# LayerNorm statistics of five token tiles as two accumulating passes on ScalarE, two more product groups in the first projection, five more warm-up matmuls

## Chip, cores, metric

One core of a Trainium2 chip. The metric is the device time of one execution in microseconds (us), the median of several runs.

## The reference, cut to what matters

```python
def _A_ref(x, wqkv, wo):                 # attention layer, linear attention, 32 heads of 32
    q, k, v = split_heads(x @ wqkv)      # x: 2048 x 1024, wqkv: 1024 x 3072
    phi = lambda t: where(t > 0, t + 1, exp(t)) + 1e-6
    pq, pk = phi(q), phi(k)
    kv, z = einsum(pk, v), sum(pk)
    return (pq @ kv / (pq @ z + 1e-6)) @ wo

x = x + _A_ref(_layernorm(x), ...)       # layer one: the only layer that the change touches
x = x + _B_ref(_layernorm(x), ...)       # gated bilinear unit
x = x + _A_ref(_layernorm(x), ...)       # layer three, same weights
x = x + _B_ref(_layernorm(x), ...)
```

## The kernel before: the parts concerned

The 2048 tokens are 16 tiles of 128. In layer one each tile is loaded, its LayerNorm statistics are taken, it is normalised and transposed, and then projected to k and q. A recorder (`P.add`) puts every operation into the in-order queue of its engine and derives the waits. The cuts below are shortened: `...` stands for dependence lists, and the loads of x and the branches for other layers are left out. The statistics take three operations on VectorE and two small ones on GpSimd:

```python
def ln_a(i):                              # statistics of tile i into mv[j]
    for h in range(2):
        P.add("dve", lambda e: e.bn_stats(st[j][:, 6*h:6*h+6], x_res[:, i, half h]), ...)
    P.add("dve", lambda e: e.bn_aggr(mv[j][:, 0:2], st[j]), ...)                     # mean, variance
    P.add("pool", lambda e: e.tensor_scalar(out=mv[j][:, 2:3], in0=mv[j][:, 1:2], scalar1=EPS_LN, op0=ALU.add), ...)
    P.add("pool", lambda e: e.tensor_tensor(out=mv[j][:, 3:4], in0=mv[j][:, 2:3], in1=mhalf, op=ALU.pow), ...)

def ln_b2(i, j, dst, ...):                # normalise: (x - mean) * rstd
    P.add("dve", lambda e: e.tensor_scalar(out=dst, in0=x_res[:, i, :], scalar1=mv[j][:, 0:1],
                                           scalar2=mv[j][:, 3:4], op0=ALU.subtract, op1=ALU.mult), ...)

def lnstep(i, h):                         # between two half projections of a tile
    if h == 0:
        lnp.start(lnp.n)                  # statistics of the next tile
        lnp.b_one()                       # normalise the one before it
    else:
        lnp.step_t(1)                     # transpose it
```

A plain projection takes 8 matmuls of 512 columns for each tile, each of k and q and each half of the columns. Its PSUM bank is evicted by an exp and a relu on ScalarE and by two operations on VectorE; four banks are used in turn. Ten tiles are projected so. For the others two tiles at a time are projected by a 2 x 2 block scheme with seven products instead of eight (28 matmuls instead of 32), which needs extra block sums and two more evictions from VectorE.

```python
PE_WARM = 10           # matmuls on zeros ahead of everything
NPL1 = 10              # tiles projected plainly; the rest in groups of seven products
LNX = (3, 5, 6)        # q projections after which a further statistics step stands
```

Of the kernel before, what the change touches and what calls it, by code (L numbers as in the profile page):

```python
# [7 lines left out]
AF = mybir.ActivationFunctionType  # L8
# [172 lines left out]
def build_kernel(nc, A_x, A_wqkv, A_wo, B_w_gate, B_w_up, B_w_down, out):  # L181
    _, S, D = A_x.shape
    F = B_w_gate.shape[1]
    NST, NSB, KT, NG, NFT, NDH = S // 128, S // 512, D // 128, D // 128, F // 128, D // 512
# [4 lines left out]
    EPS_LN = 1e-5  # L189
    PHI0 = 1e-6  # L190
    PHI1 = 1.0 + 1e-6
    PE_WARM = 10
    NHOLD = 2
    NPL1 = 10
    LNX = (3, 5, 6)
    RLB = [(4, 5, 6, 7), (4, 5, 6, 7)]
    NPE_T = 4
    NNORM = 14
# [20 lines left out]
    def take(n, align=64):  # L219
        nonlocal off  # L220
        off = (off + align - 1) // align * align
        o = off
        off += n
        return o
# [11 lines left out]
    O_MV = [take(64) for _ in range(8)]  # L236
# [21 lines left out]
    O_A = [RC + 2 * SZ_W + 1024 + i * D * 2 for i in range(2)]  # L258
# [25 lines left out]
    P = _Prog(V_TW + 8 * 32)  # L284
# [38 lines left out]
    with ExitStack() as es:  # L323
# [10 lines left out]
        def vb(o, n):  # L334
            return ab[:, o // 2: o // 2 + n]

        def vh(o, n):
            return ah[:, o // 2: o // 2 + n]

        def vf(o, n):  # L340
            return af[:, o // 4: o // 4 + n]

        x_res = vb(O_X, NST * D).rearrange("p (i d) -> p i d", d=D)
# [23 lines left out]
        xn = [vh(o, D) for o in O_XN]  # L367
        asb = [vh(o, D) for o in O_A]
        st = [vf(o, 12) for o in O_ST]
        mv = [vf(o, 5) for o in O_MV]  # L370
        pbufs = [vf(o, D) for o in O_P]
        den = vf(O_DEN, 32)
        rden = [vf(o, 32) for o in O_RDEN]
# [6 lines left out]
        def psb(b):  # L380
            return ps[:, b, :]
# [7 lines left out]
        B_KVT = [1, 2]  # L389
# [16 lines left out]
        def R(o, n):  # L406
            return [(o, o + n)]

        def r_x(i, lo=0, hi=D):
            return [(O_X + (i * D + lo) * 2, O_X + (i * D + hi) * 2)]  # L410
# [16 lines left out]
        def mset(ap, v, rng):  # L427
            P.add("pool", lambda e: e.memset(ap, v), wr=rng)

        wrm = vh(O_A[0], 512)  # L430
        mset(wrm, 0.0, R(O_A[0], 1024))
        P.add("pe", lambda e: [e.matmul(psb(B_KVT[1]), wrm[:, 0:128], wrm, start=True, stop=True) for _ in range(PE_WARM)],
              rd=R(O_A[0], 1024), pwr=[B_KVT[1]])
# [4 lines left out]
        for h in range(4):  # L438
# [4 lines left out]
              rd=R(O_IDENT, 256), wr=R(O_IDENT, 256))  # L443
        P.add("pool", lambda e: e.tensor_copy(e0, ident[:, 0:2]), rd=R(O_IDENT, 256), wr=R(O_E0, 4))

        ln_cnt = [0]

        def ln_a(i):
            j = ln_cnt[0] % 8
            ln_cnt[0] += 1  # L450
            for h in range(2):
                P.add("dve", (lambda h: lambda e: e.bn_stats(st[j][:, 6 * h:6 * h + 6], x_res[:, i, (D // 2) * h:(D // 2) * (h + 1)]))(h),  # L452
                      rd=r_x(i, (D // 2) * h, (D // 2) * (h + 1)), wr=R(O_ST[j] + 24 * h, 24))
            P.add("dve", lambda e: e.bn_aggr(mv[j][:, 0:2], st[j]), rd=R(O_ST[j], 48), wr=R(O_MV[j], 8))  # L454
            P.add("pool", lambda e: e.tensor_scalar(out=mv[j][:, 2:3], in0=mv[j][:, 1:2], scalar1=EPS_LN, scalar2=None, op0=ALU.add),  # L455
                  rd=R(O_MV[j] + 4, 4), wr=R(O_MV[j] + 8, 4))
            P.add("pool", lambda e: e.tensor_tensor(out=mv[j][:, 3:4], in0=mv[j][:, 2:3], in1=mhalf, op=ALU.pow),
                  rd=R(O_MV[j] + 8, 4) + R(O_MHALF, 4), wr=R(O_MV[j] + 12, 4))
            return j

        def ln_b1(i, j, on_act):
            if on_act:
                P.add("dve", lambda e: e.tensor_scalar(out=mv[j][:, 4:5], in0=mv[j][:, 0:1], scalar1=mv[j][:, 3:4], scalar2=-1.0,
                                                        op0=ALU.mult, op1=ALU.mult),
                      rd=R(O_MV[j], 4) + R(O_MV[j] + 12, 4), wr=R(O_MV[j] + 16, 4))
# [10 lines left out]
        class LN:  # L476

            def __init__(self, to, order):
                self.to = to
                self.order = order  # L480
                self.q_b = []
                self.q_n = []
                self.q_t = []
                self.n = 0
                self.t_next = 0
                self.use_dma = False
                self.on_act = False
# [6 lines left out]

            def start(self, i):
                assert i == self.n
                j = ln_a(self.order[i])
                self.n += 1
                self.q_b.append((i, j))

            def b1_one(self):
                if self.q_b:
                    i, j = self.q_b.pop(0)
                    ln_b1(self.order[i], j, self.on_act)
                    self.q_n.append((i, j, self.on_act))

# [169 lines left out]
        def tw_make(n, eng, parts):  # L676
            b11, b12, b21, b22 = [w_blk(n, kb, h) for kb in range(2) for h in range(2)]
            t1, t2, t3, t4 = [tw_blk(n, c) for c in (1, 2, 3, 4)]
            step = 4 // parts
            ops = []  # L680
            for o, a, b in ((t1, b12, b11), (t2, b22, t1), (t4, b21, t2), (t3, b22, b12)):
                for k in range(0, 4, step):
                    def one(o=o, a=a, b=b, k=k):
                        P.add(eng, lambda e: e.tensor_tensor(out=o[0][:, k:k + step], in0=a[0][:, k:k + step], in1=b[0][:, k:k + step], op=ALU.subtract),
                              rd=rsub(a[1], k, step) + rsub(b[1], k, step), wr=rsub(o[1], k, step))
                    ops.append(one)
            return ops
# [33 lines left out]
        def pack():  # L721
            u = pk_n[0]
            if u >= NU:
                return
            pk_n[0] += 1
            assert RG.get("n", 0) <= u, (RG["n"], u)
            j, m = unit_jm(u)
            w16 = wscr[u].bitcast(BF16)[:, 0:2048].rearrange("p (i k c) -> p i k c", i=2, c=128)
            for i in range(2):
                c0 = j * 256 + (1 - i) * 128  # L730
                dma(w16[:, i], wgu_v[m][:, :, c0:c0 + 128], R(V_PK + u * 64 + 32 * i, 32), KPK[u])
# [134 lines left out]
        def xload(i):  # L866
            dma(x_res[:, i, :], x2[i * 128:(i + 1) * 128, :], r_x(i), KX[i])

        def layer_A(lnp, nxt, first):
# [167 lines left out]
            def lnstep(i, h):  # L1037
                if h == 0:
                    if first and lnp.n < NST:
                        for t in (lnp.n, lnp.n + 1):  # L1040
                            if xnext[0] <= t < NST:
                                xload(t)
                                xnext[0] = t + 1
                    if lnp.n < NST:
                        lnp.start(lnp.n)
                    lnp.b_one()
                else:
                    lnp.use_dma = i + 1 >= NPE_T
                    lnp.step_t(1)

            if first:
                lnp.start(0)
                lnp.b_one()
                lnp.step_t(1)
                lnp.start(1)
                lnp.b_one()
            else:
                lnp.use_dma = True
            NPL = NPL1 if first else 0
            rl.update(on=first, o=O_XN[0] if first else O_XRT[tok[NST - 2]])  # L1060
            twk = []
            if first:
                twk = tw_make("k", "dve", 1)
                twq = tw_make("q", "dve", 1)
# [10 lines left out]
            for kind, i in seq:  # L1075
                for h in range(2):
                    ev = proj(kind, tok[i], h, mids.pop((kind, i, h), None) if first else None)
                    ev()
                    if lead:
                        for f in lead.pop(0):  # L1080
                            f()
                        if i == NHOLD:
                            twk.pop(0)()
                    elif kind == "k":
                        lnstep(i, h)
                if kind == "q" and len(twk) > 1:
                    twk.pop(0)()
                elif kind == "q" and i >= 1 and len(twq) > 1:
                    twq.pop(0)()
                if kind == "q" and NPL < NST and i in LNX:  # L1090
                    for h in range(2):
                        lnstep(NPE_T, h)
                if kind == "q" and i >= NPL - 2:
                    if i == NPL - 2:
                        lnp.need(NPL + 1)
                    for f in s_make(tok, NPL // 2)[2 * (i - NPL + 2):][:2]:
                        f()
                if i >= 3 and kind == "k":
                    pack()
# [19 lines left out]
            for n, (kind, p) in enumerate(items):  # L1119
# [10 lines left out]
                if first:  # L1130
                    i = NPL + len(LNX) + n
                    for j in range(2):
# [837 lines left out]
```

## Time and profile before

| | before |
|---|---|
| median, range | 1436.09 us, 1435.76 to 1439.31 (3 runs) |
| TensorE / VectorE / ScalarE busy | 99% / 85% / 47% of the span |
| first projection matmul | 8.06 us |
| third tile transposed (end) | 22.46 us |
| projections of layer one done (start of the next stage's long runs) | 115.14 us |

The page and the stages are shown in the prediction. One view is added here, because everything after it is measured with it: the chain of waits in order of time (start us, length us, what), at the end of the third transposition and at the first run of 16 matmuls of the next stage, kernel before.

```profile
22.01 0.45 PE ps L555 x8
...
115.14 3.45 PE ps L1163 x16
```

(Here and below `arena` is the SBUF memory, `ps` the PSUM banks, and the L number a line of that run's kernel.) From 22.01 + 0.45 = 22.46 to 115.14 are 92.68 us. I call this **the stage**. It holds a fixed number of 512-column matmuls, 428 before and 420 after (272 + 132 + 24 and 208 + 188 + 24 in the instruction order), so its length less 0.2158 us for each matmul is what TensorE lost to waiting: 92.68 - 92.36 = 0.3 us before.

### The profile page before, as it was taken

Reading aid. Unit: us, or ns where it says so; the run is one execution under the profiler, and the core shown is the slowest. Engines: PE = TensorE matmul, PEld = TensorE weight load, DVE = VectorE, ACT = ScalarE, POOL = GpSimd, SP = SyncE. Lnnn points to the kernel's source line nnn. Section 1 sums busy time; section 2 is a strip of 40 time slices with the busy share of each in tenths; the row PEclk is TensorE's granted clock in tenths of the full one; section 3 lists DMA queues with packets and bytes.
Section 4 is the critical chain, followed back from the end, with each engine's and each line's share of the span. In section 5 each row is a group of like instructions: output and inputs, shape, how many; then the busy total and the mean of one; then the engine's idle time right before and its main releaser. Section 6 shows DMA issues by size and latency. Waiting matters only on the chain.

```text
span 1434.8 us, 21762 instructions
## 1 busy us (share of the span) xinstructions
PE 1421.6 (99%) x8110; PEld 787.2 (55%) x8170; DVE 1213.4 (85%) x2377; ACT 676.7 (47%) x1386; POOL 148.2 (10%) x176
## 2 busy tenths in 40 slices
PE   8999999999999999999999999999999999999999
PEld 3444444555546566664544444446666475666547
DVE  7987878999988799988679978778888887888888
ACT  5672355444410266652157813667776004767400
POOL 2203621000010000002000045310000100000000
PEclk9999999999999999999999999999999999999999
DMA  6778978997796777768893266767776976777653
GB/s 206 165 201 232 216 175 197 303 300 266 255 267 210 238 253 256 247 235 297 235 285 97 89 172 163 181 181 255 263 242 194 289 255 225 259 260 258 206 192 120
DMA packets 272586, 320.73 MB, mean 224 GB/s; under 512 B 164064, under 2 KB 215008, under 8 KB 272480
## 3 DMA queue, kind: packets, MB, share of 16 engines
q1 hardware_dynamic: 272480, 319.34, 72.7%
q8 instruction: 64, 1.05, 0.3%
q14 instruction: 42, 0.34, 0.1%
HBM read 236.45 MB, written 73.40 MB: 216 GB/s over the span
## 4 chain that ended last, share of the span: by engine, by line
PE 91%; DVE 5%; issue 1%; ACT 1%; DMA 1%; SPq 0%; POOL 0%; POOLq 0%; DVEq 0%
PE ps L1347 28%; PE ps L1428 17%; PE ps L1764 14%; PE ps L1265 8%; PE ps L1163 8%; PE ps L897 6%; PE ps L929 5%; PE ps L1682 5%; DVE arena L767 3%; DVE arena L770 1%; DMA arena<-arena 1%; PE ps L1189 1%; PE ps L1216 0%; DVE arena L949 0%; DVE arena L452 0%
## 5 line engine op out<-in xcount | busy, mean ns | idle before, releaser
L767 DVE TENSOR_TENSOR arena<-arena 128x512 f16<-128x512 f16 (+9 forms) x1015 | 497.8, 518 | 59.6 <-ACT arena L1432 34.1
L1347 PE MATMUL ps<-arena 128*128 128x512 f16 x1888 | 457.0, 379 | 0.9 <-DVE arena L770 0.9
L770 DVE SCALAR_TENSOR_TENSOR arena<-ps,arena 128x512 f16<-128x512 f32 (+3 forms) x545 | 353.9, 664 | 68.1 <-PE ps L1764 28.4
L1428 PE MATMUL ps<-arena 128*128 128x256 f16 x2184 | 287.5, 273 | 1.0 <-DVE ps L1441 1.0
L1347 PEld LDWEIGHTS ps<-arena 128*128 128x128 f16 (+1 forms) x1888 | 183.0, 98 | 163.3 <-ACT ps L1376 3.8
L1428 PEld LDWEIGHTS ps<-arena 128*128 128x128 f16 (+1 forms) x2184 | 212.2, 98 | 91.6 <-ACT arena L1432 6.9
L1764 PE MATMUL ps<-arena 128*128 128x512 bf16 (+1 forms) x1102 | 242.8, 379 | 1.0
L1764 PEld LDWEIGHTS ps<-arena 128*128 128x128 f16 x1120 | 109.5, 98 | 130.5 <-DVE arena L767 0.5
L1352 ACT ACTIVATE arena<-ps 128x512 f32<-128x512 f32 x224 | 133.7, 597 | 76.5 <-PE ps L1347 61.6
L1432 ACT ACTIVATE arena<-ps 128x256 f32<-128x256 f32 x351 | 125.1, 384 | 26.9 <-PE ps L1428 22.0
L929 PE MATMUL ps<-arena 128*128 128x512 f16 (+1 forms) x551 | 122.2, 379 | 1.0 <-ACT arena L936 0.4
L1163 PE MATMUL ps<-arena 128*128 128x512 bf16 x498 | 114.7, 379 | 0.7
L1265 PE MATMUL ps<-arena 128*128 128x512 bf16 x502 | 110.3, 379 | 0.5
L455 POOL TENSOR_SCALAR arena<-arena 128x1 f32<-128x1 f32 x64 | 24.7, 386 | 816.8 <-DVE arena L454 816.8
L1438 ACT COPY ps<-ps 128x256 f32<-128x256 f32 x182 | 66.4, 365 | 74.9 <-DVE arena L770 29.3
L1376 ACT COPY ps<-ps 128x512 f32<-128x512 f32 x112 | 65.4, 584 | 64.1 <-PE ps L1347 52.1
L452 DVE BATCH_NORM_STATS2 arena<-arena 128x6 f32<-128x512 bf16 x128 | 88.2, 689 | 6.6 <-DMA arena<-in_A_x_dram 4.3
L1031 POOL TENSOR_TENSOR arena<-arena 128x1024 f16<-128x1024 f32 x32 | 76.9, 2404 | 158.4 <-DVE arena L1029 147.2
L929 PEld LDWEIGHTS ps<-arena 128*128 128x128 f16 x560 | 54.0, 98 | 68.2 <-ACT arena L936 5.7
L897 PE MATMUL ps<-arena 128*128 128x512 bf16 x375 | 86.1, 384 | 1.5 <-DVE arena L549 0.5
L1682 PE MATMUL ps<-arena 128*128 128x256 f16 (+1 forms) x784 | 86.8, 273 | 0.7 <-DVE arena L770 0.5
L1441 DVE TENSOR_TENSOR ps<-ps,arena 128x256 f32<-128x256 f32 x182 | 76.7, 428 | 10.5 <-PE ps L1428 9.6
(62 smaller groups left out, 900.9 us busy)
## 6 DMA issues: line engine op xcount, KB each, us to landing
arena<-w_scratch SPq DMA_DIRECT2D x84, 896.0 KB, 4.6
arena<-t_scratch SPq DMA_DIRECT2D x32, 896.0 KB, 6.1
arena<-in_B_w_down_dram SPq DMA_DIRECT2D x24, 896.0 KB, 5.4
arena<-sp_scratch SPq DMA_DIRECT2D x26, 768.0 KB, 4.4
w_scratch<-arena SPq DMA_DIRECT2D x28, 512.0 KB, 6.1
arena<-w_scratch SPq DMA_DIRECT2D x28, 384.0 KB, 4.8
x_scratch<-arena SPq DMA_DIRECT2D x40, 256.0 KB, 7.2
arena<-x_scratch SPq DMA_DIRECT2D x40, 256.0 KB, 5.6
```

What stands on the lines that cost most here:

```text
L767: P.add("dve", lambda e: e.tensor_tensor(out=out, in0=a, in1=b, op=op), rd=rd, wr=wr, prd=prd)
L770: P.add("dve", lambda e: e.scalar_tensor_tensor(out=out, in0=a, scalar=sc, in1=b, op0=ALU.mult, op1=op1), rd=rd, wr=wr, prd=prd)
L897: P.add("pe", (lambda ks: lambda e: [e.matmul(psb(bank), xnT[:, k, i * 128:(i + 1) * 128], t[:, k, h * 512:(h + 1) * 512], start=(k == 0), ...
L929: P.add("pe", lambda e: [e.matmul(psb(bank), a[0][:, k, :], b[0][:, k, :], start=(q in (1, 5) and k == 0), stop=(k == 3), skip_group_check ...
L1163: return [e.matmul(psb(bank), xrt[t][:, jj * 128:(jj + 1) * 128], pk[:, h, t, :], start=(t == tok[0]), stop=(t == tok[NST - 1])) for t in ts]
L1265: return [e.matmul(psb(bank), xnT[:, g, i * 128:(i + 1) * 128], wp[:, g, dh * 512:(dh + 1) * 512], start=(dh == 0 and g == 0), stop=(g == ...
L1347: P.add("pe", lambda e: [e.matmul(psb(bank), w[:, k, :], x[:, k, :], start=(start and k == 0), stop=(k == 3), skip_group_check=True) for k ...
L1352: P.add("act", lambda e: e.activation(t, psb(bank), AF.Copy, scale=SG), prd=[bank], wr=r)
L1428: P.add("pe", lambda e: [e.matmul(psb(bank)[:, 256 * half:256 * half + 256], w[:, k, :], xx[:, k, :], start=(start and k == 0), stop=(k == ...
L1432: P.add("act", lambda e: e.activation(d, src, AF.Copy, scale=sc), prd=[xk], wr=rd_)
L1682: P.add("pe", lambda e: [e.matmul(psb(bank)[:, 256 * half:256 * half + 256], a[:, k, 128 * r:128 * r + 128], b[:, k, :], start=(start and ...
L1764: P.add("pe", lambda e: [e.matmul(psb(bank), hv[:, 7 * hf + k, t * 128:(t + 1) * 128], w[:, k, :], start=(q in "15" and hf == 0 and k == 0 ...
```

## The change

Its intent: project two more tiles with seven products, and make room for them on VectorE by taking the statistics of tiles 5, 7, 9, 11 and 13 as two passes with a summing output on ScalarE; keep TensorE's clock up with more warm-up matmuls. GpSimd negates the mean between the passes.

```diff
-    PE_WARM = 10
+    PE_WARM = 12
-    NPL1 = 10
-    LNX = (3, 5, 6)
+    NPL1 = 8
+    LNX = (1, 3, 4)
+    LN_ACT = (5, 7, 9, 11, 13)
...
+        def ln_s1(i, dst, r_dst):
+            P.add("act", lambda e: e.activation(dst, x_res[:, i, :], AF.Copy, scale=1.0 / D, accum_out=mv[j][:, 0:1]), ...)
+            P.add("pool", lambda e: e.tensor_scalar(out=mv[j][:, 5:6], in0=mv[j][:, 0:1], scalar1=-1.0, op0=ALU.mult), ...)
+        def ln_s2(i, j, dst, r_dst):
+            P.add("act", lambda e: e.activation(dst, x_res[:, i, :], AF.Square, bias=mv[j][:, 5:6], scale=1.0, accum_out=mv[j][:, 6:7]), ...)
+            P.add("pool", lambda e: e.tensor_scalar(out=mv[j][:, 2:3], in0=mv[j][:, 6:7], scalar1=1.0 / D, scalar2=EPS_LN, op0=ALU.mult, op1=ALU.add), ...)
+            ln_rstd(j)
...
             def start(self, i):
-                j = ln_a(self.order[i])
+                if self.to == "A0" and i in LN_ACT:
+                    j = ln_s1(self.order[i], *self.dst(i)); self.q_s.append((i, j))
+                else:
+                    j = ln_a(self.order[i])
...
                 else:
+                    lnp.s2()                                  # second pass, half a tile's projection later
                     lnp.step_t(1)
...
                 lnp.step_t(1)
+                P.add("pe", lambda e: [e.matmul(psb(B_KVT[1]), wrm[:, 0:128], wrm, ...) for _ in range(3)], ...)
```

Left out: x tiles are loaded five instead of two steps ahead, and the remaining weight block sums are flushed before the last plain projections.

More of the change, by code (lines that the diff above doesn't have):

```diff
@@ L369, in build_kernel @@
         st = [vf(o, 12) for o in O_ST]
-        mv = [vf(o, 5) for o in O_MV]
+        mv = [vf(o, 8) for o in O_MV]
         pbufs = [vf(o, D) for o in O_P]
@@ L456, in ln_a, with ln_rstd @@
                   rd=R(O_MV[j] + 4, 4), wr=R(O_MV[j] + 8, 4))
+            ln_rstd(j)
+            return j
+        def ln_rstd(j):
             P.add("pool", lambda e: e.tensor_tensor(out=mv[j][:, 3:4], in0=mv[j][:, 2:3], in1=mhalf, op=ALU.pow),
                   rd=R(O_MV[j] + 8, 4) + R(O_MHALF, 4), wr=R(O_MV[j] + 12, 4))
-            return j
+        def ln_s1(i, dst, r_dst):
+            j = ln_cnt[0] % 8
+            ln_cnt[0] += 1
+            P.add("act", lambda e: e.activation(dst, x_res[:, i, :], AF.Copy, scale=1.0 / D, accum_out=mv[j][:, 0:1]),
+                  rd=r_x(i), wr=r_dst + R(O_MV[j], 4))
+            P.add("pool", lambda e: e.tensor_scalar(out=mv[j][:, 5:6], in0=mv[j][:, 0:1], scalar1=-1.0, scalar2=None, op0=ALU.mult),
+                  rd=R(O_MV[j], 4), wr=R(O_MV[j] + 20, 4))
+            return j
+        def ln_s2(i, j, dst, r_dst):
+            P.add("act", lambda e: e.activation(dst, x_res[:, i, :], AF.Square, bias=mv[j][:, 5:6], scale=1.0, accum_out=mv[j][:, 6:7]),
+                  rd=r_x(i) + R(O_MV[j] + 20, 4), wr=r_dst + R(O_MV[j] + 24, 4))
+            P.add("pool", lambda e: e.tensor_scalar(out=mv[j][:, 2:3], in0=mv[j][:, 6:7], scalar1=1.0 / D, scalar2=EPS_LN, op0=ALU.mult, op1=ALU.add),
+                  rd=R(O_MV[j] + 24, 4), wr=R(O_MV[j] + 8, 4))
+            ln_rstd(j)
         def ln_b1(i, j, on_act):
@@ L481, in __init__ @@
                 self.q_b = []
+                self.q_s = []
                 self.q_n = []
@@ L496, in start, with s2 @@
                 assert i == self.n
-                j = ln_a(self.order[i])
+                if self.to == "A0" and i in LN_ACT:
+                    j = ln_s1(self.order[i], *self.dst(i))
+                    self.q_s.append((i, j))
+                else:
+                    j = ln_a(self.order[i])
                 self.n += 1
                 self.q_b.append((i, j))
+            def s2(self, upto=NST):
+                while self.q_s and self.q_s[0][0] <= upto:
+                    i, j = self.q_s.pop(0)
+                    ln_s2(self.order[i], j, *self.dst(i))
             def b1_one(self):
@@ L503, in b1_one @@
                     i, j = self.q_b.pop(0)
+                    self.s2(i)
                     ln_b1(self.order[i], j, self.on_act)
@@ L1039, in lnstep @@
                     if first and lnp.n < NST:
-                        for t in (lnp.n, lnp.n + 1):
+                        for t in range(lnp.n, lnp.n + 5):
                             if xnext[0] <= t < NST:
@@ L1054, in layer_A @@
                 lnp.step_t(1)
+                P.add("pe", lambda e: [e.matmul(psb(B_KVT[1]), wrm[:, 0:128], wrm, start=True, stop=True) for _ in range(3)],
+                      rd=R(O_A[0], 1024), pwr=[B_KVT[1]])
                 lnp.start(1)
@@ L1085, in layer_A @@
                         lnstep(i, h)
+                if kind == "q" and i == NPL - 3:
+                    for f in twk + twq[:-1]:
+                        f()
+                    twk, twq = [], twq[-1:]
                 if kind == "q" and len(twk) > 1:
```

## The prediction

> **What bounds the kernel now.** I began with the page of the profiled execution, its busy shares and its chain of waits.
>
> ```profile
> PE 1421.6 (99%) x8110; PEld 787.2 (55%) x8170; DVE 1213.4 (85%) x2377; ACT 676.7 (47%) x1386; POOL 148.2 (10%) x176
> ...
> PE 91%; DVE 5%; issue 1%; ACT 1%; DMA 1%; SPq 0%; POOL 0%; POOLq 0%; DVEq 0%
> ```
>
> TensorE is busy for 1421.6 of 1434.8 us and is 91% of the chain that ended last. So only two things can move the time: fewer or faster matmuls, or some of the 13 us in which TensorE stands still. The change touches only the first attention layer, so I cut that layer into stages: to the first projection, to the second token tile, the rest of the start, the plain projections, and the projections done as seven products.
>
> ```profile
> 0.00:8.06 8.06, 4.59 (x19) 1.72 (x19) 2.57 (x5) 1.87 (x2) 3.01 (x18) 1.00 0.76 238
> 8.06:14.07 6.01, 5.77 (x25) 2.16 (x25) 3.62 (x8) 2.16 (x4) 0.79 (x2) 0.72 1.08 360
> 14.07:22.46 8.39, 8.10 (x48) 4.04 (x50) 7.00 (x17) 5.52 (x10) 1.84 (x4) 1.00 0.78 265
> 22.46:81.16 58.70, 58.38 (x267) 26.62 (x272) 55.27 (x128) 36.48 (x69) 16.14 (x24) 1.00 0.73 161
> 81.16:115.14 33.98, 33.79 (x155) 15.09 (x156) 29.53 (x71) 25.84 (x47) 0.00 (x0) 1.00 0.65 194
> ```
>
> The columns are the stretch and its length, then busy time of PE, PEld, DVE, ACT and POOL, the granted TensorE clock, DMA share and GB/s. From 22.46 on TensorE is full. The instruction order has 272 matmuls of 512 columns between the third transposition and the first seven-product group, and they take 58.70 us: 215.8 ns each. In the same stretch VectorE is busy 55.27 us, 94%, yet TensorE loses nothing to it: four PSUM banks lie between them. In the product stage the program has 140 matmuls of the products and 16 of the next stage up to 115.14; 156 x 0.2158 = 33.67 us of 33.98, so 0.3 us is lost. The clock of 0.72 in the second stretch is the other feature.
>
> Then I read the start in order of time:
>
> ```profile
> 1.36 3.97 PE L432 MATMUL ps<-arena 128*128 128x512 f16 x10 [1.36 <-POOL arena L428]
> ...
> 6.92 0.62 PE L547 MATMUL ps<-arena 128*128 128x128 f16 x8 [1.58 <-DVE arena L472]
> ...
> 8.06 4.46 PE L897 MATMUL ps<-arena 128*128 128x512 bf16 x12 [0.52 <-DVE arena L549]
> ...
> 11.12 0.55 DVE L472 TENSOR_SCALAR arena<-arena 128x1024 f16<-128x1024 bf16 x1 [1.00 <-POOL arena L457]
> 11.46 0.56 PEld L897 LDWEIGHTS ps<-arena 128*128 128x128 f16 x4 [0.74 <-DMA arena<-in_A_wqkv_dram]
> ...
> 12.35 0.61 PE L555 MATMUL ps<-arena 128*128 128x128 f16 x8
> ```
>
> Ten warm-up matmuls end at 5.33, TensorE idles to 6.92, transposes tile 0, and begins to project at 8.06. Its weight loads are then 0.43 us apart, half rate, until about 11.5. But the ninth projection matmul needs the second half of the k weights, and its weight load is released by that transfer at 11.46, with the DMA engines saturated (share 1.08). The eight slow matmuls end at 8.06 + 8 x 0.427 = 11.48. The slow clock is thus almost exactly hidden behind the weight transfer.
>
> **What the Trainium skill says.** "TensorE: Matmul & The Clock Gate", section "Back-to-back issue gap" with the part on the clock gate: a 512-column matmul costs N/2.4 + 2.5 ns warm, 215.7 ns measured, and 426.7 ns cold. This trace agrees: 215.8 and about 427 ns. The same page, section "What's actually happening": the clock is decided over free-running windows of 3.4 us, so where the change of rate falls differs from run to run. Here it is granted half between about 8.1 and 11.6 us, one window. I infer that the thin stretch from 5.33 to 8.06 caused it. "ScalarE: Activation LUTs", section "What ACT_TABLE_LOAD costs": 186 ns + 0.833 ns per element, and some 93 ns more for each per-partition operand. For 1024 elements with two such operands that gives 1225 ns; the trace's normalisations on ScalarE take 1240. The same page, section "Table sets: the hidden batching unit", says cheap functions sit in every set; the changed program still has one table load, so Square and Copy cost no switch. No page that I read prices the accumulating output; I take it as free.
>
> **The change part by part.**
> *Seven products for tiles 8 to 11.* Eight instead of ten tiles are projected plainly. A plain pair of tiles costs 2 x 2 x 8 = 32 matmuls, a product group 7 x 4 = 28. Two more groups (k and q of tiles 8, 9) save 8 matmuls: the order shows 272 + 132 become 208 + 188. TensorE is full there, so 8 x 0.2158 = 1.73 us lies on the path. Although four k pairs are product groups afterwards, three of them were already.
> *Statistics.* Five tiles lose two BATCH_NORM_STATS2 (0.71 us each when back to back) and an aggregation (0.21): 5 x 1.63 = 8.2 us off VectorE. The two new groups add there two L949 evictions each (4 x 0.686 = 2.7) and one pair's four operand sums (4 x 0.42 = 1.7). Net -3.8 us: (55.27 + 29.53 - 3.8) / (92.7 - 1.7) = 89% instead of 91%. ScalarE gains ten passes, an estimate from the ScalarE page of 1039 ns (immediates) and 1133 ns (one operand), 5 x 2.17 = 10.9 us. Each group costs it 4 evictions as exp and relu at 0.6 halved (2.4), three copies at 0.58 and two exps at 0.72, 5.6 us, against 4.8 for plain: +1.6 for two. (36.48 + 25.84 + 12.5) / 91 = 82%, up from 67%. Neither engine is full. This part saves no time by itself; it pays for the products.
> *Order.* For four of the five tiles the second pass stands one projection, some 1.7 us, ahead of the normalisation that uses it. For tile 5 the normalisation follows at once, so VectorE may wait 1 to 2 us there, which the banks absorb. The forced finishing of the weight sums before the last plain projections and the deeper x loads fill engines with room: the DMA share is 0.06 from 20 to 25 us.
> *Warm-up.* Two more warm-up matmuls fall into the idle 1.58 us and three more between transposition and projection: 3 x 0.216 = 0.65 us against an idle 0.52, or 1.28 us if cold. If they hold the clock, the first eight projections take 1.73 us instead of 3.42, but then TensorE waits for the weights until 11.46 all the same. Tile 1 is not normalised before 11.12 + 0.55 = 11.67 either. I count 0.0 us gained.
> Sum: -1.73 + 0 + 0.2 for small stalls in a longer product stage = -1.5 us; 1436.09 - 1.5 = 1434.6, and I take 1434.5.
>
> **The rivals.**
> *ScalarE or VectorE becomes the bound.* The last groups have to share VectorE with the statistics of tiles 14 and 15 (3.3 us) and three normalisations. For: VectorE works 29.53 of 33.98 us already. Against: layer three does fifteen such groups along with statistics, and its stretch reads
>
> ```profile
> 731.40:826.40 95.00, 94.10 (x430) 41.99 (x436) 85.01 (x211) 75.25 (x136) 4.97 (x11) 1.00 0.46 134
> ```
>
> where 436 weight loads x 0.2158 = 94.1 of 95.0 us: 0.9 us lost over fifteen groups, so about 0.4 over seven. Were in-order ScalarE to hold up PSUM banks while it waits on GpSimd between passes, 2 to 3 us would be lost and the time would be 1436 to 1437.
> *The clock drops later.* A warm start would end its eight matmuls near 9.9 and idle to 11.46. If the window that ends near 11.6 then counts as idle, the next 3.4 us run at half rate, with about 1.2 us of it exposed: 1435.7. Such a drop after an even longer gap is seen in the kernel before.
> *The start gains.* If weights land earlier in most executions than in the one profiled, a warm clock could give up to 8 x 0.213 = 1.7 us: 1432.8. The saturated DMA and the tile-1 normalisation speak against it.
>
> **Range and chances.** The three timed runs of before already span 1435.76 to 1439.31. From the rivals' 1432.8 and 1437 with noise I take 1432.3 to 1436.8. Two per cent is 28.7 us; the layer portion touched is 115 us and no engine in it is overloaded, so a change past 2% either way has a chance of one in a hundred.
>
> **What would show it.** Right: 208 plain matmuls after the third transposition at 215 to 216 ns, then 188 in product groups with under 1 us lost; the ninth projection matmul again released near 11.4 by the weight transfer; VectorE near 89% and ScalarE near 82% from there to the end of the groups; every later stage earlier by one constant. Wrong: TensorE waits on ScalarE or VectorE lines of over 1 us in all between 25 and 115 us, passes on ScalarE well above 1.2 us, half clock after 11.6 us, or the first projection of tile 1 starting well before 14.07.

## The result, and the profile after

| | before | after |
|---|---|---|
| median (range), runs | 1436.16 us (1435.76 to 1439.31), 4 | 1435.57 us (1434.92 to 1435.93), 4 |
| span of the profiled run | 1434.8 us | 1433.9 us |
| the start: third transposition ends | 22.46 us | 22.21 us |
| the stage | 92.68 us | 92.22 us |
| from the stage to the end | 1319.66 us | 1319.47 us |
| VectorE / ScalarE busy in the stage | 91% / 67% | 89% / 80% |

The ratio is 0.9991, 95% interval 0.9973 to 1.0008: the same. Here and below a ratio is the mean time of one kernel's fast runs over that of the other's in the same rounds, so not quite the ratio of the quoted medians. The last three time rows account for the traces' 0.9 us: 0.25 in the start, 0.46 in the stage, 0.19 after it, the last only as exact as the spans, which are given to 0.1 us.

The page of the changed kernel, busy shares and chain by engine:

```profile
PE 1420.6 (99%) x8107; PEld 786.8 (55%) x8167; DVE 1209.5 (84%) x2370; ACT 688.2 (48%) x1408; POOL 149.9 (10%) x181
...
PE 84%; DVE 8%; ACT 2%; DMA 2%; issue 2%; POOL 1%; SPq 1%; POOLq 0%; DVEq 0%; ACTq 0%
```

TensorE's busy time fell by 1.0 us (the five added warm-up matmuls count in it), and its share of the chain from 91% to 84%: the chain now runs through VectorE, ScalarE and GpSimd for a while. The stage in the changed kernel's chain of waits:

```profile
21.76 0.45 PE ps L586 x8
...
114.43 3.45 PE ps L1201 x16
```

114.43 - 22.21 = 92.22 us for 420 matmuls, which need 90.64. TensorE loses 1.6 us there, not 0.3. TensorE's own timeline of the changed kernel shows where (start, length, what, idle before and its releaser):

```profile
22.05 17.43 PE L928 MATMUL ps<-arena 128*128 128x512 bf16 x78
39.91 24.55 PE L928 MATMUL ps<-arena 128*128 128x512 bf16 x110 [0.43 <-ACT arena L658]
64.82 3.63 PE L928 MATMUL ps<-arena 128*128 128x512 bf16 x15 [0.36 <-ACT arena L658]
68.29 40.96 PE L960 MATMUL ps<-arena 128*128 128x512 bf16 x185
```

The kernel before has one unbroken line of 58.87 us in that place. Here the plain projections stand still until 39.9 and again until 64.8 us, and weight loads waited until 57.4 as well, each time for L658, the relu that empties a PSUM bank. The product groups after 68.29 run without a stop. What kept ScalarE is seen in the timeline of all engines around tile 11:

```profile
50.50 1.14 ACT L468 ACTIVATE arena<-arena 128x1024 f16<-128x1024 bf16 x1
51.45 0.28 ACT L468 ACTIVATION_READ_ACCUMULATOR arena<-arena 128x1 f32 x1
...
52.75 0.21 DVE L455 BATCH_NORM_AGGREGATE arena<-arena 128x2 f32<-128x12 f32 x1
...
53.05 0.56 POOL L456 TENSOR_SCALAR arena<-arena 128x1 f32<-128x1 f32 x1 [3.89 <-DVE arena L455]
...
53.69 0.77 POOL L462 TENSOR_TENSOR arena<-arena 128x1 f32<-128x1 f32 x1
...
54.55 0.53 POOL L470 TENSOR_SCALAR arena<-arena 128x1 f32<-128x1 f32 x1
...
55.11 1.15 ACT L475 ACTIVATE arena<-arena 128x1024 f16<-128x1024 bf16 x1 [2.41 <-POOL arena L470]
...
57.37 0.55 PEld L928 LDWEIGHTS ps<-arena 128*128 128x128 f16 x4 [0.52 <-ACT arena L658]
```

The first pass (L468) has its sum at 51.73. The negation (L470) is ready to run, but GpSimd takes its instructions in order and the two before it belong to tile 10, whose statistics come from VectorE and are aggregated only at 52.75 + 0.21 = 52.96. So the negation begins at 54.55, and ScalarE, also in order, stands 2.41 us before its second pass (L475). The evictions behind that pass are late, and at 57.37 TensorE has no free bank. Over the stage ScalarE stood 4.4 us so, in three of the five tiles (who waited for whom: us in total, times, longest us):

```profile
ACT arena L475 <- POOL arena L470: 4.4, 3, 2.4
```

These waits end at 37.64 (tile 7, 0.72 us), 55.11 (tile 11, 2.41 us) and 62.56 us (tile 13, 1.27 us), and each of TensorE's three stops ends 2.26 to 2.27 us later, at 39.91, 57.37 (there a weight load) and 64.82. Before the second passes of tiles 5 and 9 ScalarE stood under 0.1 us, and no such stop follows them.

The start, TensorE's timeline of the changed kernel:

```profile
1.37 5.30 PE L433 MATMUL ps<-arena 128*128 128x512 f16 x12 [1.37 <-POOL arena L429]
6.46 0.92 PE L578 MATMUL ps<-arena 128*128 128x128 f16 x8
7.21 0.81 PE L1087 MATMUL ps<-arena 128*128 128x512 f16 x3
7.90 1.90 PE L928 MATMUL ps<-arena 128*128 128x512 bf16 x8
11.23 1.04 PE L928 MATMUL ps<-arena 128*128 128x512 bf16 x4 [1.44 <-DMA arena<-in_A_wqkv_dram]
```

The first eight projection matmuls run at full rate, 1.90 us, and TensorE then stands 1.44 us for the weights, as predicted. The 0.25 us won goes with the weights' earlier arrival, 11.23 instead of 11.46.

### The profile page after: what moved, and what is told of

The parts are those of the page before. It is cut to its first block, busy times and chain, and to the rows that moved or that the text cites. A ratio compares the mean times of both kernels' runs of the same rounds, so it can differ in the third digit from the quotient of the medians.

```text
span 1433.9 us, 21771 instructions
## 1 busy us (share of the span) xinstructions
PE 1420.6 (99%) x8107; PEld 786.8 (55%) x8167; DVE 1209.5 (84%) x2370; ACT 688.2 (48%) x1408; POOL 149.9 (10%) x181
## 4 chain that ended last, share of the span: by engine, by line
PE 84%; DVE 8%; ACT 2%; DMA 2%; issue 2%; POOL 1%; SPq 1%; POOLq 0%; DVEq 0%; ACTq 0%
PE ps L1385 28%; PE ps L1466 17%; PE ps L1802 14%; PE ps L1201 8%; PE ps L960 6%; PE ps L1720 5%; PE ps L1303 4%; DVE arena L798 3%; PE ps L928 2%; DMA arena<-arena 1%; DVE arena L453 1%; DVE arena L801 1%; DMA arena<-in_A_wqkv_dram 1%; ACT arena L658 1%; SPq L426 1%
## 5 line engine op out<-in xcount | busy, mean ns | idle before, releaser
L798 DVE TENSOR_TENSOR arena<-arena 128x512 f16<-128x512 f16 (+9 forms) x1019 | 498.8, 517 | 60.1 <-ACT arena L1470 34.2
L1802 PEld LDWEIGHTS ps<-arena 128*128 128x128 f16 x1120 | 109.5, 98 | 130.4 <-DVE arena L798 0.4
L960 PE MATMUL ps<-arena 128*128 128x512 f16 (+1 forms) x606 | 134.1, 379 | 1.0 <-ACT arena L967 0.4
L1201 PE MATMUL ps<-arena 128*128 128x512 bf16 x498 | 114.7, 379 | 0.7
L1303 PE MATMUL ps<-arena 128*128 128x512 bf16 x502 | 110.3, 379 | 0.5
L456 POOL TENSOR_SCALAR arena<-arena 128x1 f32<-128x1 f32 x59 | 20.8, 353 | 806.8 <-DVE arena L455 806.8
L960 PEld LDWEIGHTS ps<-arena 128*128 128x128 f16 x616 | 59.5, 98 | 74.7 <-ACT arena L967 5.8
L453 DVE BATCH_NORM_STATS2 arena<-arena 128x6 f32<-128x512 bf16 x118 | 81.3, 689 | 5.4 <-DMA arena<-in_A_x_dram 3.3
L1303 PEld LDWEIGHTS ps<-arena 128*128 128x128 f16 x512 | 50.1, 98 | 60.4
```

The lines of the kernel that those rows point to most:

```text
L453: P.add("dve", (lambda h: lambda e: e.bn_stats(st[j][:, 6 * h:6 * h + 6], x_res[:, i, (D // 2) * h:(D // 2) * (h + 1)]))(h), rd=r_x(i, (D ...
L798: P.add("dve", lambda e: e.tensor_tensor(out=out, in0=a, in1=b, op=op), rd=rd, wr=wr, prd=prd)
L960: P.add("pe", lambda e: [e.matmul(psb(bank), a[0][:, k, :], b[0][:, k, :], start=(q in (1, 5) and k == 0), stop=(k == 3), skip_group_check ...
L1201: return [e.matmul(psb(bank), xrt[t][:, jj * 128:(jj + 1) * 128], pk[:, h, t, :], start=(t == tok[0]), stop=(t == tok[NST - 1])) for t in ts]
L1303: return [e.matmul(psb(bank), xnT[:, g, i * 128:(i + 1) * 128], wp[:, g, dh * 512:(dh + 1) * 512], start=(dh == 0 and g == 0), stop=(g == ...
L1802: P.add("pe", lambda e: [e.matmul(psb(bank), hv[:, 7 * hf + k, t * 128:(t + 1) * 128], w[:, k, :], start=(q in "15" and hf == 0 and k == 0 ...
```

## The experiments

Twelve further runs were made, ten of them of new kernels and two repeats; all results were correct. They came in three batches, each on one chip, with the kernel before timed in each. Its medians there were 1436.73, 1437.39 and 1436.39 us, so times are compared within a batch only. The diffs are shortened (`pool:` stands for one operation on GpSimd). Differences of a few tenths are read from the traces' stage, which repeats to 0.02 us, as the next table shows.

| kernel | plain tiles | median us | ratio to before, 95% interval | third transposition ends | the stage | TensorE's loss in it |
|---|---|---|---|---|---|---|
| after, again | 8 | 1436.78 | 1.0002 (0.9988 to 1.0016) | 22.09 | 92.21 | 1.6 |
| neg | 8 | 1434.57 | 0.9986 (0.9973 to 0.9998) | 22.11 | 90.76 | 0.1 |
| neg_now | 8 | 1434.01 | 0.9981 (0.9968 to 0.9993) | 21.95 | 90.76 | 0.1 |
| all_dve | 8 | 1438.28 | 1.0010 (0.9998 to 1.0023) | 22.39 | 94.29 | 3.7 |
| pool_twice | 8 | 1436.70 | 1.0000 (0.9986 to 1.0013) | 22.25 | 92.94 | 2.3 |
| stats_only | 10 | 1437.78 | 1.0006 (0.9993 to 1.0019) | 23.68 | 92.49 | 0.1 |
| old_warm | 8 | 1436.24 | 0.9994 (0.9981 to 1.0006) | 21.83 | 92.22 | 1.6 |
| cold | 8 | 1436.17 | 0.9993 (0.9981 to 1.0006) | 22.27 | 92.20 | 1.6 |
| before, again | 10 | 1436.55 | 1.0000 (0.9982 to 1.0018) | 22.40 | 92.68 | 0.3 |
| warm_only | 10 | 1437.17 | 1.0003 (0.9991 to 1.0016) | 24.24 | 92.68 | 0.3 |
| neg_oldwarm | 8 | 1434.43 | 0.9985 (0.9972 to 0.9999) | 22.24 | 90.76 | 0.1 |
| npl6 | 6 | 1439.26 | 1.0021 (1.0008 to 1.0034) | 23.50 | 94.59 | 5.7 |

The loss is the stage less 0.2158 us for each of its matmuls: 428, 420 or 412 with ten, eight or six plain tiles.

### The wait between the passes, or the work of the passes?

**The changed kernel again**, for a second trace.

> The changed kernel itself, for a second trace on the chip of the variants. Theory W (TensorE is stopped because ScalarE waits on GpSimd between its two passes): from the third transposition to the first long run of the next stage 420 matmuls of 512 columns take 92.2 us again, 1.5 to 1.6 us over 420 x 0.2158 = 90.6; half of the product gain of 1.73 us is lost there. Time 1435 to 1436 us. Theory S (the 0.25 us won at the start is only where the weight transfer happened to land): the ninth projection matmul starts somewhere between 11.1 and 11.6 us, not always at 11.23.

The stage took 92.21 us again, and the ninth projection matmul started at 11.11. Theories W and S both hold so far; the expected time of 1435 to 1436 us was missed. In this batch the changed kernel was as fast as before (1436.78 against 1436.73), so its advantage of the first measurement, 0.6 us, is not resolved by timed runs; only the 0.46 us of the stage are certain, from two traces of each kernel.

**neg** takes GpSimd out from between the passes and leaves their work:

```diff
-  e.activation(dst, x_res[:, i, :], AF.Copy, scale=1.0 / D, accum_out=mv[j][:, 0:1])
-  pool: mv[j][:, 5:6] = mv[j][:, 0:1] * -1.0
+  e.activation(dst, x_res[:, i, :], AF.Copy, scale=-1.0 / D, accum_out=mv[j][:, 5:6])
   # normalisation of these five tiles: add mv[5] instead of subtracting mv[0]
```

> The changed kernel with the first pass scaled by -1/1024, so that its accumulator is the negated mean, the second pass takes it as bias directly, and GpSimd's negation between the passes is gone; the normalisation adds instead of subtracting. ScalarE's load stays. Theory W: ScalarE's waits on GpSimd (4.4 us in the changed kernel) vanish, and TensorE's loss between 22 and 114 us falls from 1.6 to 0.5 us or less; time 1.0 us under the changed kernel, 1434.5 us. Rival L (it is the 12.5 us of extra work on ScalarE, not the wait): the loss stays at 1.3 us or more and the time stays at 1435.5 us.

TensorE's timeline of neg:

```profile
21.94 45.06 PE L930 MATMUL ps<-arena 128*128 128x512 bf16 x208
66.83 40.85 PE L962 MATMUL ps<-arena 128*128 128x512 bf16 x188
```

The 208 plain matmuls are one unbroken run now, and the stage falls from 92.21 to 90.76 us; the time falls by 2.2 us against the changed kernel of the same batch, of which the stage explains 1.45 and the rest is within the scatter of the runs. ScalarE's waits on GpSimd are gone from the list of waits. VectorE's waits for GpSimd's reciprocal roots are not: 3.3 us in the stage, the longest 1.9, in the changed kernel and in neg alike. So these are not what stopped TensorE, although GpSimd has less to do in neg.

**neg_now** in addition puts the second pass directly behind the first:

```diff
   self.q_s.append((i, j))
+  self.s2(i)
```

> As neg, and the second pass follows the first at once instead of one projection later. Theory W': the first of the three stops (near 39.9 us) comes from tile 5, whose normalisation on VectorE follows its second pass too closely; with both passes together the reciprocal root is ready a projection earlier and this stop goes too: loss 0.3 us or less, 1434.3 us. Rival L: two passes in a row hold ScalarE for 2.4 us, so PSUM banks come free later and the loss is as in neg or greater.

The stage is the same, 90.76 us, so my special theory for tile 5 falls: the stop at 39.9 us had gone with the GpSimd wait alone. VectorE still waits 1.9 us there in neg and 0.5 at most in neg_now, but TensorE feels neither. The two ScalarE loads, from the view by stretches over the stage, first the changed kernel, then neg_now:

```profile
22.21:114.43 92.22, 90.87 (x413) 40.64 (x420) 81.67 (x191) 73.45 (x138) 16.42 (x29) 1.00 0.70 166
```

```profile
21.95:112.71 90.76, 90.76 (x421) 40.91 (x420) 81.51 (x191) 74.24 (x138) 14.84 (x24) 1.00 0.74 170
```

ScalarE (fourth busy column) works 73.45 us in the first and 74.24 us in the second, in a shorter stretch, and TensorE loses nothing. Rival L, the load, is refuted. This version is faster than both kernels, though by less than the 2% that counts as a change: 1434.01 us, 0.19% under before.

**pool_twice** lengthens the suspected wait instead: GpSimd first copies the mean, then negates the copy.

```diff
-  pool: mv[5] = mv[0] * -1.0
+  pool: mv[7] = mv[0] * 1.0
+  pool: mv[5] = mv[7] * -1.0
```

> The changed kernel with GpSimd's negation of the mean done in two steps (a copy, then the negation): the wait between ScalarE's passes is longer by one small operation, 0.25 to 0.6 us a tile, everything else as it was. Theory W (that wait is what stops TensorE): ScalarE's waits on GpSimd rise from 4.4 to 6 us or more and TensorE's loss from the third transposition to the next stage rises from 1.6 to 2.2 to 3.0 us. Rival: the banks absorb half a microsecond, the loss stays at 1.6 us.

ScalarE's waits on GpSimd rose from 4.4 to 6.2 us and TensorE's loss from 1.6 to 2.3 us. Theory W holds from both sides. The growth is in the early tiles: the wait of tile 7 grows from 0.72 to 1.21 us, and TensorE's idle time 2.27 us after it from 0.43 to 0.92 us. Tile 5 waits 1.22 us now, without a visible stop after it, and for tiles 11 and 13 the wait is as before (2.44 and 1.31 us). The timed runs do not resolve the 0.7 us. Which share of the wait is GpSimd's own operations and which its standing behind the neighbouring tile's statistics was not separated by a run; for tile 11 the lines above give it: of the 3.38 us from the sum to the second pass, 1.3 pass until tile 10's aggregation has been released to GpSimd at 53.05, and the rest is three small operations with their gaps.

### Did the statistics have to leave VectorE, and do they cost by themselves?

**all_dve** leaves all statistics on VectorE, with everything else as changed:

```diff
-    LN_ACT = (5, 7, 9, 11, 13)
+    LN_ACT = ()
```

> The changed kernel with all statistics on VectorE as before; products, order and warm-up stay. By my sums VectorE then has 81.1 + 8.2 = 89 us of work in 91 us of TensorE work, 98%. Theory V (the statistics had to leave VectorE for the products to pay): TensorE loses more than 1.6 us between 22 and 114 us, by waits on VectorE lines, and the time is 1436 to 1437.5 us, no better than before. Rival B (four PSUM banks absorb it): the loss is under 0.8 us and the time 1434.5 to 1435 us, better than the changed kernel, so moving the statistics was not needed.

TensorE's timeline of all_dve:

```profile
22.22 36.84 PE L928 MATMUL ps<-arena 128*128 128x512 bf16 x168
59.80 8.81 PE L928 MATMUL ps<-arena 128*128 128x512 bf16 x40 [0.75 <-ACT arena L658]
68.54 1.04 PE L960 MATMUL ps<-arena 128*128 128x512 bf16 x4
71.37 40.12 PE L960 MATMUL ps<-arena 128*128 128x512 f16 x184 [1.79 <-DVE arena L798]
```

Theory V holds: 3.7 us lost, most of it where the first product group waits at 71.37 for a VectorE line (L798), and 1438.28 us, above the expected range. VectorE is busy 88.4 of 94.3 us in the stage, 94%, as in the plain projections before, where TensorE lost nothing. Here the block sums must be ready at one point, and an average over the stage does not show that. Whether another order with all statistics on VectorE would have kept up was not tried.

**stats_only** has the two passes with GpSimd between them, but ten plain tiles, the old `LNX` and the old warm-up; the deeper loads of x and the early flush of the weight sums stay:

```diff
-    NPL1 = 8;  LNX = (1, 3, 4)
+    NPL1 = 10; LNX = (3, 5, 6)       # and PE_WARM = 10, no three between
```

> The kernel before with its ten plain tiles and its ten warm-up matmuls, and only the statistics of five tiles on ScalarE by two passes. Theory W: the wait on GpSimd stops TensorE here as well, 0.5 to 1.5 us lost in the plain projections where the kernel before lost 0.3 us in all, so the kernel is 0.3 to 1.2 us slower than before. Rival P (the stops come only with the tighter order of the product groups): loss 0.3 us, time as before.

The stage took 92.49 us for 428 matmuls, 0.1 us lost, with 2.0 us of ScalarE waits on GpSimd. They are two, of 0.72 and 1.27 us, as long as those ahead of the changed kernel's stops at 39.9 and 64.8 us. So theory W in the form that any such wait stops TensorE is wrong, and for waits of this length rival P is right: with ten plain tiles and the old order they cost nothing. A wait of 2.4 us did not occur here, and which part of the order gives the slack was not separated. Timed, it does not differ from before (1437.78 against 1437.39 us, interval around 1). That its trace is longer by more (a span of 1436.6 us, 1.8 more than before) comes largely from its start, 1.2 us, as the next part shows, and not from the stage.

### The clock at the start

Four runs change the warm-up: **old_warm** (the changed kernel with the warm-up of before), **cold** (with a single warm-up matmul), **warm_only** (the kernel before with only the five new ones), **neg_oldwarm** (neg_now with the warm-up of before). **before_again** is a second look at before.

```diff
 old_warm, neg_oldwarm:  PE_WARM = 12 -> 10, the three matmuls after the transposition removed
 cold:                   PE_WARM = 12 -> 1,  the three removed
 warm_only:              the kernel before with PE_WARM = 10 -> 12, the three added
```

> The changed kernel with the ten warm-up matmuls of before and without the three between transposition and projection. Theory H (the weight transfer hides the slow clock): the clock falls to half again for one window near 8 us, the eight projection matmuls take 3.4 us instead of 1.7, and the ninth still starts between 10.97 and 11.6 us; stages after it unchanged, time within 0.4 us of the changed kernel. Rival G (the warm-up gains): the ninth starts 0.5 us or more later than 11.23, time 0.5 to 1.7 us more.

> The changed kernel with one warm-up matmul. Theory H: the transpositions and eight projection matmuls run at half rate and end near 11.8 us, 0.3 to 0.6 us later than the weights; after that half rate goes on [...]to some point from 11.8 to 15 us, which costs at most 1.5 us more. Time 0.5 to 2 us over the changed kernel. Rival: no difference beyond 0.3 us.

> The kernel before with only the five added warm-up matmuls. Theory H: no gain in a start where the half-rate window falls under the weight transfer, third transposition at 22.0 to 22.5 us, stage of 92.7 us unchanged, time equal to before within 0.4 us in most executions. Rival D (the warm-up guards against a half-rate window after 11.4 us, as one of the traces with ten warm-ups had it): some executions of before are about 1.3 us longer and none of this one; the mean falls by 0.3 to 1.0 us.

> The variant without GpSimd between the passes and with both passes together, but with the ten warm-up matmuls of before. Stage of 90.8 us as in that variant. Theory H: 2.0 to 2.7 us under before, like that variant. Rival D: 1.0 to 1.7 us under before on average, with some executions 1.3 us longer than others.

> The kernel before itself, for a second trace of its start. If the half clock falls where it will: the stage from the third transposition to the next stage takes 92.7 us again, but the third transposition may end anywhere from 21.8 us (no half-rate window, or a hidden one) to 23.7 us (a half-rate window after the weights have come). Time 1436 to 1437.5 us.

Theory H holds in the main. With a single warm-up matmul TensorE's timeline reads

```profile
7.81 4.51 PE L928 MATMUL ps<-arena 128*128 128x512 bf16 x12 [0.52 <-DVE arena L580]
```

at half rate until the weights come, and yet the third transposition ends at 22.27 us, against 22.21 and 22.09 in the changed kernel. I expected 0.5 to 2 us of harm and missed: the full rate came just as the weights did. (The granted clock misleads here: in this trace it stands at 1.00 from 8 to 11 us, while the weight loads are 0.43 us apart.) The old warm-up in the changed kernel (21.83 us) and in neg_now (22.24 us) does no harm either; old_warm did not even show the half-rate window that I expected of it, and its ninth projection matmul started at 10.85 us, earlier than expected, while neg_oldwarm did show the window, from 7.7 to 11.1 us, hidden. before_again came as expected (92.68 us, 22.40, 1436.55 us); warm_only did not, as its third transposition, expected at 22.0 to 22.5 us, came at 24.24. Of the five traces with ten warm-up matmuls, the two that idled 1.58 and 1.28 us ahead of the first transposition had the half-rate window near 8 us, and the three that idled 0.5 to 1.0 us had not. That agrees with what the prediction inferred of the thin stretch, but is no test of it.

The late half-rate window, my second rival, does exist. It came with old and new warm-up alike. TensorE's timeline of stats_only:

```profile
7.46 1.90 PE L928 MATMUL ps<-arena 128*128 128x512 bf16 x8 [0.52 <-DVE arena L580]
11.45 1.49 PE L928 MATMUL ps<-arena 128*128 128x512 bf16 x4 [2.09 <-DMA arena<-in_A_wqkv_dram]
12.73 1.06 PE L586 MATMUL ps<-arena 128*128 128x128 f16 x8
```

The eight matmuls run warm, then TensorE waits 2.09 us for the weights, and the granted clock is half from just before 12 to about 15 us. The third transposition ends at 23.68 us. The same happened in warm_only (idle 2.56 us, 24.24) and npl6 (2.01 us, 23.50), both with the new warm-up. The other traces whose eight matmuls ran warm idled 1.2 to 1.9 us and kept the clock (third transposition at 21.83 to 22.40). So rival D, that the added matmuls guard against this, is not borne out: two of eight traces with them, one of five with ten of the old kind. It may make part of the 1 to 3.5 us by which timed runs of one kernel differ, but those runs have no trace, so that stays open.

### Further in the same direction

**npl6** projects only six tiles plainly, on the base of neg_now:

```diff
-    NPL1 = 8;  LNX = (1, 3, 4)
+    NPL1 = 6;  LNX = (0, 1, 2, 3)
```

> The variant without GpSimd between the passes and with both passes together, and six plain tiles instead of eight: two more product groups, 8 matmuls fewer. If the other engines keep up, the stage takes 90.8 - 1.7 = 89.0 us and the kernel is 1.7 us faster than that variant, some 4 us under before. By the sums VectorE then has 85.5 us of work in 89, 96%, so a loss of 1 us or more on VectorE lines is the rival, with no gain left over the eight-tile variant.

It is slower than before, 1439.26 us. One wait carries most of the 5.7 us of loss, in TensorE's timeline of npl6:

```profile
59.28 53.64 PE L963 MATMUL ps<-arena 128*128 128x512 f16 x240 [3.84 <-DVE arena L801]
```

As in all_dve, the first product group waits for its block sums from VectorE. The rival came true, larger than expected. An order with the sums earlier was not tried.

## Why the prediction was right, and where it was not

The measured 1435.57 us lie in the range and in "the same"; the point, 1434.5, was 1.1 us too low. That the time fell into the range is in part luck: the range of 4.5 us also holds the time of the kernel before, 1436.16 us, and the changed kernel's median of the second measurement, 1436.78 us, lies at its very edge. The predicted gain of 1.5 us was not reached.

- **Seven products, -1.73 us: right.** 208 and 188 matmuls stand in the trace, and when nothing stops TensorE (neg) the stage is 92.68 - 90.76 = 1.92 us shorter: the 1.73 and 0.2 us of the small loss of before.
- **"0.2 for small stalls in a longer product stage": the step that failed.** It measured 1.6 - 0.3 = 1.3 us, and not in the product stage, which runs without a stop, but in the plain projections, where TensorE stopped three times for the ScalarE line L658: the prediction's own sign of being wrong, more than 1 us of such waits, came true. I had asked how far ahead of its use the second pass stands ("some 1.7 us, ahead of the normalisation"), and not what the second pass itself waits for: a GpSimd operation that stands in order behind the neighbouring tile's statistics on VectorE. Room ahead of the normalisation was there: in the trace 3.0 to 9.2 us lie between the end of the second pass of tiles 7, 9, 11 and 13 and their normalisation, more than the 1.7 I had counted, and at tile 5 VectorE waited 1.88 us, as foreseen. My first rival named the wait that cost and put the loss at 2 to 3 us; it is half of that. (The sum there was also off: 2 to 3 us over 1434.5 are 1436.5 to 1437.5, not 1436 to 1437.)
- **Loads: right as sums, not sufficient.** VectorE was to be 89% busy and is 81.67 / 92.22 = 89%; ScalarE 82% and is 73.45 / 92.22 = 80%. Neither number says that TensorE will stop, or where.
- **Passes priced from the Trainium skill**, "ScalarE: Activation LUTs": 1039 and 1133 ns estimated, 1082 and 1154 ns mean measured. But "I take it as free" of the summing output was wrong: each is followed by an ACTIVATION_READ_ACCUMULATOR of 226 and 194 ns mean, 2.1 us in all on ScalarE. With 20% of ScalarE free it did not matter.
- **No extra table load: right**, one ACT_TABLE_LOAD as before.
- **Warm-up, 0.0 us: right.** The clock held and TensorE waited for the weights; in the one trace of it, one warm-up matmul served as well as fifteen. The 0.25 us won at the start are within the spread of the weight transfer, which lets the ninth matmul begin (its weight load, in the first of them) at 11.46 and 11.41 us in two traces of before, at 11.23 and 11.11 in two of after.
- **Second rival, the clock dropping after 11.6 us**, put at 1.2 us: seen in three traces of fourteen, which moved the third transposition from 22.2 us, the mean of the eleven others, to 23.5 to 24.2 us, but not in the changed kernel's own two.

With the measured 1.3 us in place of the 0.2 the sum would have been -1.73 + 1.3 = -0.4 us in the stage; the traces have -0.46. Later stages start earlier by nearly one constant, as predicted: 0.71 us at the end of the stage and 0.68 us at the same point of layer three (821.37 us before, 820.69 after), 0.9 at the end.

## What to carry to other kernels

When work moves to an engine with room, count not only its load there but every wait that the move puts into that engine's in-order queue: a one-column operation on a third engine between two passes cost most of what the change had won, and folding the sign into the first pass's scale gave it back. Busy shares of 80 and 89% neither promise nor forbid a stop; ask which operation stands in front of the one needed, on each engine of the chain. And before warming a clock, see what the first fast matmuls will wait for next.

## What the Trainium skill lacked or had wrong

- "ScalarE: Activation LUTs" names the accumulator output but does not price it: in the trace it is an instruction of its own, ACTIVATION_READ_ACCUMULATOR, 0.18 to 0.30 us.
- "TensorE: Matmul & The Clock Gate", section "Why this matters for your kernels", advises against idle gaps of more than about 3 us. Here gaps of 2.0, 2.1 and 2.6 us after eight warm matmuls were followed by half rate for about 3.4 us; gaps of 1.2 to 1.9 us were not. One gap per trace is compared; whether its length decides or where it falls was not separated.
- The same page's section "Back-to-back issue gap" gives some 131 ns at 512 columns for the "real kernel" stream of weight loads and matmuls, and says that its formula for a single matmul (some 216 ns) over-counts there. This kernel loads weights for every matmul, and 272 in a row took 215.8 ns each: the formula, not the 131 ns.
